# Four V copies of one attention unit move from VectorE to ScalarE, with a new stored instruction order

## The chip, the cores and the metric

The kernel runs on one core of a Trainium2 chip. The metric is the device time of one execution in microseconds (us). The engines are named as in the profile: PE (TensorE, matrix products), PEld (its weight loads), DVE (VectorE), ACT (ScalarE), POOL (GpSimd) and SP (SyncE, which here only issues DMAs).

## The reference

Two independent layers whose outputs are joined along the last axis. S = 2048 tokens, D = 640 channels, all in bf16.

```python
# A: a short filter, a gate, a long convolution over the tokens, a gate
k_shift = sum(k_pad[:, t:t+S, :] * shift_k[:, 3-t] for t in range(4))
kv = k_shift * v
y = irfft(rfft(kv, 2*S) * rfft(ssm_k, 2*S))[:, :S] + kv * ssm_D
a = q * y
# B: attention of 32 heads of 20 channels, in 4 segments of 512 tokens, with a memory
for s in range(4):
    p = softmax(qs @ ks.T * scale + causal_mask)
    a_dot = p @ vs
    a_mem = (phi(qs) @ M) / (phi(qs) @ z + 1e-6)
    o = g * a_mem + (1 - g) * a_dot
    M = M + phi(ks).T @ vs;  z = z + phi(ks).sum()
b = concat(o) @ wo
out = concat([a, b], axis=-1)
```

## The kernel before

**Layer A** is done in five convolutions of 128 channels each, `conv(dp)` with dp = 0 to 4. The filter and the gated input are transformed by matrix products with a table (`Wf`), ACT copies the products out of PSUM into the tile `F`, and DVE does the last butterflies (`Kh`, `Xh`), the complex product (`pq`, `Y`) and the first butterflies back. The inverse transform is again matrix products (`Y` with `Wi`). DVE multiplies the result by q (`outa`, or `vt` for the last convolution), and POOL issues its output DMA.

**Layer B** is done in eight units: unit u covers segment s = u // 2 and half = u % 2 of the heads (16 heads). Per unit:

- `project(u)`: PE multiplies the turned input `xT` by `wqkv`, in four blocks of 128 tokens. ACT copies K and Q of each block into `KQ`; V of each block is copied into `Va` by ACT or DVE. SP issues a DMA transposition of `KQ` into `KQT` for each block. `KQT` and `Va` exist once for each half, so unit u+2 writes over those of unit u. phi of K and Q is made by an exponential on ACT (`PP`) and two operations on DVE (`qabs`, `PP`); phi of Q is transposed by DMA into `PqT`. Then DVE reduces `KQT` to the largest key of each head and channel (`kam`, 2.28 us for one), makes the matrix `A` from it, PE multiplies it by |Q|, and ACT copies the product, a bound on the logits, into `bT`. Four small DMAs put it into spare rows of `KQT`.
- `attend(u)`: for four groups of four heads PE makes the logits in fills of 4 x 512 columns (below the diagonal, on it, and one joined fill for two groups), ACT takes the exponential of each fill in two instructions of 128 x 1024 (`ET`), PE multiplies by `Va` and by the memory `Mbd`, and DVE divides (`rr`, `o`, `o_s`).
- `project_out(s)`, once a segment is done: SP issues DMA transpositions of `o_s` into `xT`, PE multiplies by `wo`, the result is copied into `outb` (`kT` for the last segment) and written out.

**The order.** None of this runs in the order in which it is written. The functions only record operations; each one is kept with its engine and with the PSUM group that it uses. `ORDER` is a stored permutation of the 1501 operations and `BASE` the PSUM bank of each of the 470 groups; `rec.issue(order, base)` (lines 244 and 842) then emits the operations in that order. Every engine and every DMA queue works through its own part of the order strictly in sequence: an instruction that has to wait holds up all that stand behind it on the same engine. All instructions carry line 253 in the profile, the line of `issue` that emits them, so they are told apart by tile.

The engine that copies V is chosen in `project` by the list `LATE_V`:

```python
769  LATE_V = (6, 7)
590  self.evict(u in LATE_V, Va[:, t, :, 0:DH], g.ap[:, 0, 0:320].rearrange("p (h d) -> p h d", d=DH), g)
```

`evict` (line 351) emits a copy on DVE where its first argument is true, and on ACT otherwise. With `LATE_V = (6, 7)` the V copies of the last two units, eight of 32, are on DVE.

Of the kernel before, what the change touches and what calls it, by code (L numbers as in the profile page):

```python
# [21 lines left out]
S = 2048; D = 640  # L22
H = 32; DH = 20; NS = 4; L = 512
# [238 lines left out]
class Layer:  # L262
# [306 lines left out]
    def project(self, u):  # L569
# [5 lines left out]
        for t in range(4):  # L575
# [11 lines left out]
            with rec.one():  # L587
                for cc in range(5):
                    nc.tensor.matmul(g.ap[:, 0, 0:320], lhsT=xT[:, cc, tok], rhs=self.wqkv[:, cc, half, 2, :], start=(cc == 0), stop=(cc == 4), grp=g)
            self.evict(u in LATE_V, Va[:, t, :, 0:DH], g.ap[:, 0, 0:320].rearrange("p (h d) -> p h d", d=DH), g)  # L590
            rec.key = ("KT", u, t)
# [174 lines left out]
PEX = ()  # L766
TURNED = (0,)
LATE_W = (2, 3)
LATE_V = (6, 7)
EARLY_K = ()  # L770
EARLY_SK = (0, 1, 2)
PARTS = (0, 3, 4, 5)
SK_ACT, X_ACT, W_SP = (), False, ()
KQW, FW, WW = 1, 1, 1
ORDER = r"""
c-jrq(_$D16a>(ji@Hs1JGE`wscqY~ZQDt0+qP}n+Wmy{aMB_gq60{W^hkk-NQqR)fQ(3uKxD>r%!FVD0uUFGpol3EK*WRLD=Hy8qM|Y!X^;SkkreTf5Sfq!iBJ{EPzAA&9I+%0Vj~B#AO>P0C$b`~
q?268jcmw{<dQ<ZA%P^6ERt1X%Xegxl#)u)NFqrrMNkyQP#h&t5~WZYd5{<RkROFm7zI!eWl$Dzq&!kfpk$Qvl0h;_IV6+nsEy201JzImL8ysZNFqrkuEdjysDQ?3g63#})@XyesE2uIiulqD*`+=j
Ag4q|4rz!+C?EwT6k4Jc2FO5Zi+0E*xuvI!lU~vR?a>j1Bs2!eco{665C%~&Tt>(=>5SgeN2W?w43VKST}H|%nIIG8rc9E_l2^(~c_}BOWsKyJ?~+gQ%P{#NpQOKhmIyjU>PZ8sFF)m%bVEe#EB$1w
bb)IqEiB#914X2m%*I^I!3>!tGo=@z>j(KLs;1#Iy!J$Il#((s3;$%cKo`m)`GGmIK;{cIsxF4;JSi<jWwFf10))j9MA5mj6w9y>i_jO*v=4@&f>e}BvJsoG9wFF(eu$xKFaR-iIaXj8VrfHZEd4PU
#igW_kVaBNR-&fVlFitHfv7C2P(`XrH3^a?(o|NXnbejc7>?>vM+PAnYw-(pWdxebI&8%@w2<xCfnC^%FVa@pNqcE2t)z{N!e5E39b`XROGoJ>f3O<|aR_^H8l9z!bd_$h4+rpDzR42lE@AZy4&w-p  # L780
<0npF502tDj$tHD;uLzwSE<fO8lY!!4u2%B#@6#_pbfQ=#?i*QM!M)axqypUE1k5nhSo6JRa@$6X{GHnSbAzN?X5|)xhB;RX`%7-654Arjjstbu_n?EI#B!QXpBKe9ghi^gaJB8*UMx~!DS>=klY{}
<)Hk<KOB}7as@)8Q+XAKWR<LxrLs)IVTbILv6zTmvRn2@ZHD4<3C%DJ%c;1ANDN>&MrL?MXB0+dH13sYh`{Tp!-%|ro2bWIxQ$J+Pd3XI*(%%QF=BAP9Fe*_APw1w<8V}t$tgJ_+vN_9OMg8p=cFmm
%LVD7&GZRQ%Ly5xC#9R-Lk7Kz%W_4o$~76R8TF#H*6x}~oACiI$#uDpHhM#D$s^R~L&Rh(rqwu1%=Fqs8?y=1X#+OZq)f)x9I8nek8#;nQ?joP*O8i#XY?r&v7g?SVfqX&@Eq}(oGCN~Q|bu4C-)_}
zQik}W-6xAJ91ajFf9X_j_Fy0HThVc$U}J`kL0OjU`A$QX3eTubSFpYXdSO(^t=Ahe+nC`U-g@&)<Dh7G@6B3`Ba~2Exy5PY-LNn(YM;1Eg0IeX?D$_t(a4D=_mcD9odPw^|K~mdv;)6?aX|dUkhkK
&7+013yWw`eT#Q^j}IuOAMpvF@depAPP4Hs+p#OVvACAd!dg=Q=xcc+fAy8V)*Q^qvRY2x$~$Sz-E6}>%*EWy!%|vCcd@kQ<70iIFQmLy(3k&Lcl)jHw6a#ws#;AyXhof%m9(bT(%Sk(^RhUL@udW5
9j&X?)$Ex(msb+X!dMNhr|&hawXwEVUuj}fbec}o{A_BIG@^yKf}E-mteMT#`8rPvuqeY>5kA)!TFrv2idD5*R*1E2md@68*52l5b8BJKb*Ap+KF-iOR@Wj~fJL#W7TF5(r$)2I`b(E+H(RR9bh%E}
7241m*#cdtWmuMtZIPB>NtWh%U8SpaqXz4H3DFJOoojTHZq_ZjQrBuP9_A75(4E?Y`+0y>Se~U=mAiDSZr5$PTU%RC_GTY;v3`th`*gn^(1RMpz8ua&x>tvCogUU|+@nYJm>$;?+Q2$nSL<#gIG96t
QipLQNAZZB(jInN%W)t_Glq@fAok|~j^#FPXH6T&@tnZwc1~kj4U1>-t)A7l1lGaMYDa5nt?VEVF}v-ziOgY>nA1901@7P!PUdaBqepp+6<L{;IF&c`mfqF#oW@=@oxSZWFYp{svxyz&3|{0Jp5P_M
wm25odfF9zWeM%7zP9^z%@SE+dtle?hTXJ_n#3+?GCQvq^s?TydzRGtSYJEI%e<!jY!*-Px+b?+Hj}eCmrrdDm+^_Ev<I5P<}sC}wm=(XX>6eNw<}C*>1=>K)O&hgAL$EwX?g92=Ck~^fEg^KWwOkc
#nM|=o6jZuXrHWr6|_ZM%!RzlYrMgwyv|!JWH<TV3fl)OYQ;U5J+`}iXGN^6m9z48$8y_aK4b-}XnE|JeYav(+)CJ2D{0^Cxs|dfe9cGvVLvUKm9`RohxhoD&sfsm@FicdkQeq+{+usZ#wyuu4!4mu  # L790
!hTsTukBU5s+aRW_S-7keLmn=8)wUT%Wm5WuHs+&XK=dsO1|Y_8)BpEJ;&QSF1HUHZDVXL*Kq@<*>sy>Gi^PG+ALFFX`eXEX4^-W_tgyM8isI%O|Xf!k(;=gTlj@@tb#Z2NjBN0*i>6$%dC>mwRtw*
7T7{tWR-oXt+LhjnZfqP-dYW>=^?h(KHFD*V*y`h)xE6O^TqbXesGO#v`x0zw%AtNU<JLHueZ=1#=moi?X+FC+ba4t`^i1F-S*l(J78hGng@A(59bm5p*^yO-pIpyWRK#%S;y<T`9b^jKiwp%yBG1M
9?FY)L=W)N9?6q<GH>in{D?*K=pMskdKo`zNj;Xw_Bj5B&Ahp{_Ez4~TX-r@?QuPx$M*!D&=Yxb5A@@9!u~R)pR`k!-cxuc&+J(|t0(php3$>;8qe-I{E!{CbbieK5t7!sdUwz1xjeV$@w}eT^LsaM
<Lx|@gqE-}(l1+EALXO{qP6!9E~0YD!U-k3M3e~9$vgTL>*789v~~8V5=Np)bm{GVys!83{yxA5`U>yqy?l(1^+7(^m-!GM>cf1vkMkHZ-p|-XziP{Ul27oJKEkK?S&JkA5?P|iRG;iKe5TLx**?eT
`aGZJ)BT*Ev-5Vr=KBI)=!<-@2m2bo?x%dMpZC)q;+K7$FY%>*)Q|ZV-{k9ktKaa0e#p1^W<Tz${Dg1!Gk(~Q_-eo67yPDQ^=p38Z}|q_=zDyx@9>?z&oBB}-{t%Lw(s^!e!%|&2dC=h
"""
BASE = r"""
c-mD{0g?kD2#bL5{~sTQ==SOq9fSahyK#Po!0zQdCyI8rH`-TyvbMpKWA)vM0r!)6{K>nMk@ProvaQpG@Jf4jzB6jIXX)PQU2Ufdh-JM8Yk-jl*J)R;d%qY_vd)f;y(e>w)n-m-SH-x=HD-cSZFYRP
Fk*zxAP#s+?Q;%xvc=u>mYk&I!^6C|Ar3!mh_6v&`kVQ;c%GON=fl~DF?^X+G-;dMU5w-Lmf~_4OQ{v=G5Al-|M3C(L$URA-JE(fAO7YYq%<F9UFesG_=h|1DaDqvx2ayQPh+JU|Mi>7wugFo#$zU^
w@d5P)blnMnW;DTR)3e-c#4Orq^i2KSX?2cN|AUI;k~BRo57FnkTUo6FXG;>??nFrVeSTj  # L800
"""


# [69 lines left out]
```

## Time and profile before

| | |
|---|---|
| median of the timed runs | 292.07 us (291.34, 292.07, 292.85) |
| the profiled execution | 292.63 us |
| its span, first to last instruction | 290.9 us |
| mean granted TensorE clock | 0.998 |
| DVE busy | 263.3 us, 402 instructions |
| PE busy | 257.5 us, 4219 instructions |
| ACT busy | 252.1 us, 387 instructions |
| PEld busy | 193.1 us |
| POOL busy | 44.1 us |
| exponentials of the logits on ACT | 160 of 1064 ns |
| copies of V: ACT, DVE | 24 of 457 ns, 8 of 484 ns |

Busy time is the time in which an engine had at least one instruction under way. Instructions of one engine overlap at their ends, so the durations of a group add up to more than the engine's busy time. The span is that of one profiled execution; the rest of its 292.63 us lies around the first and last instruction.

### The profile page before, as it was taken

To read this page: it belongs to the slowest core of one execution; us is meant where nothing else is said; L and a number is where in the kernel's file an instruction comes from. 1 tells how busy PE (TensorE), PEld (TensorE's weight loads), DVE (VectorE), ACT (ScalarE), POOL (GpSimd) and SP (SyncE) were. 2 spreads that over 40 slices of the span, in tenths; PEclk is the share of its full clock that TensorE was granted. 3 is DMA by queue.
4 is the path that set the end of the run, shared out by engine and by line. 5 is a ranking of instruction groups with operands and counts; after the bars stand their busy time and mean duration, and the time that the engine had idled before them with its cause. 6 is when DMAs were issued, how large, how long until landed. Compare 5 with 4: busy or idle time off the path is not lost. (4 is left out here: it accounts for less than half of the span.)

```text
span 290.9 us, 9864 instructions
## 1 busy us (share of the span) xinstructions
PE 257.5 (89%) x4219; PEld 193.1 (66%) x4226; DVE 263.3 (91%) x402; ACT 252.1 (87%) x387; POOL 44.1 (15%) x71
## 2 busy tenths in 40 slices
PE   0899998889998989999889989999888887799895
PEld 0687765768677767787756777657756665476773
DVE  1279999999999999999999999999999999899654
ACT  0593899899998997999989989999989899899963
POOL 8300000001005000333000320201001400001620
PEclk9999999999999999999999999999999999999999
DMA  6999989996938498993794159983490119911332
GB/s 182 375 239 168 240 145 199 141 246 129 165 104 211 95 164 169 193 180 111 116 190 83 54 81 143 215 128 87 78 179 23 38 35 143 192 39 34 106 77 100
DMA packets 113500, 40.71 MB, mean 140 GB/s; under 512 B 105696, under 2 KB 111376, under 8 KB 113328
## 3 DMA queue, kind: packets, MB, share of 16 engines
q1 hardware_dynamic: 108624, 34.07, 60.9%
q0 software_dynamic: 2064, 4.76, 6.3%
q10 hardware_dynamic: 2768, 1.24, 1.5%
q8 instruction: 33, 0.54, 0.8%
q14 instruction: 11, 0.09, 0.1%
HBM read 14.11 MB, written 5.24 MB: 67 GB/s over the span
## 5 line engine op out<-in xcount | busy, mean ns | idle before, releaser
L253 ACT ACTIVATE ET<-ps 128x1024 bf16<-128x1024 f32 x160 | 155.8, 1064 | 6.8 <-PE ps L253 5.9
L253 PEld LDWEIGHTS <-xT 128*128 128x128 bf16 x640 | 59.7, 98 | 34.6 <-issue 12.2
L253 PE MATMUL ps<-wqkv,xT 128*128 128x320 bf16 x480 | 75.6, 303 | 4.7 <-ACT ET L253 1.4
L253 POOL DMA_DIRECT2D out_dram<-outa x32 | 22.4, 848 | 172.4 <-DVE outa L253 169.3
L253 ACT CAST F<-ps 128x512 bf16<-128x512 f32 x80 | 43.6, 628 | 4.9 <-DVE F L253 1.9
L253 PEld LDWEIGHTS <-ET 128*128 128x128 bf16 x1296 | 40.3, 96 | 3.9 <-issue 2.0
L253 PE MATMUL ps<-Va,ET 128*128 128x21 bf16 x1280 | 40.9, 172 | 0.7 <-ACT ET L253 0.5
L253 PE MATMUL ps<-KQT 32*128 32x128 bf16 (+2 forms) x896 | 35.0, 239 | 3.4 <-DVE o_s L253 1.0
L253 PEld LDWEIGHTS <-Wf 128*128 128x128 bf16 x320 | 29.9, 97 | 6.6 <-issue 2.3
L253 ACT CAST KQ<-ps 128x320 bf16<-128x320 f32 x64 | 27.4, 470 | 3.9 <-PE ps L253 2.6
L253 PE MATMUL ps<-wo,xT 128*128 128x320 bf16 x160 | 25.7, 299 | 2.3 <-DMA xT<-o_s 1.4
L253 PEld LDWEIGHTS <-KQT 32*128 32x128 bf16 x896 | 16.5, 92 | 14.2 <-issue 12.6
L253 PE MATMUL ps<-vt,Wf 128*128 128x256 bf16 x160 | 20.6, 272 | 0.7 <-DVE vt L253 0.7
L253 PE MATMUL ps<-kT,Wf 128*128 128x256 bf16 x160 | 20.9, 272 | 0.2 <-ACT F L253 0.2
L253 PE MATMUL ps<-Y,Wi 128*128 128x256 bf16 x160 | 20.3, 273 | 0.8 <-ACT ET L253 0.4
L253 PE MATMUL ps<-mright,mleft 32*128 32x128 bf16 x512 | 15.1, 216 | 6.3 <-ACT ET L253 3.0
L253 DVE TENSOR_TENSOR o<-ps,rr 128x640 bf16<-128x640 f32 x24 | 19.7, 820 | 0.7
L253 PE MATMUL ps<-skd,kr 128*128 128x128 bf16 (+3 forms) x133 | 19.0, 286 | 1.1 <-issue 0.4
L253 PEld LDWEIGHTS <-kr 128*128 128x128 bf16 x140 | 17.1, 145 | 3.7 <-issue 0.7
L253 PE MATMUL ps<-Mbd,PqT 128*128 128x84 bf16 x96 | 18.0, 201 | 0.8 <-ACT bT L253 0.4
L253 DVE TENSOR_TENSOR Y<-Y,pq 128x2048 bf16<-128x2048 bf16 (+1 forms) x20 | 18.7, 946 | 0.0
L253 DVE TENSOR_TENSOR pq<-Xh,Kh 128x2048 bf16<-128x2048 bf16 x15 | 18.3, 1218 | 0.3
(77 smaller groups left out, 359.3 us busy)
## 6 DMA issues: line engine op xcount, KB each, us to landing
vt<-in_A_v_dram SPq DMA_DIRECT2D x10, 256.0 KB
pq<-in_A_q_dram SPq DMA_DIRECT2D x10, 256.0 KB
out_dram<-outa POOLq DMA_DIRECT2D x32, 64.0 KB, 2.4
out_dram<-outb POOLq DMA_DIRECT2D x12, 160.0 KB, 2.6
ET<-in_A_ssm_k_dram SPq DMA_DIRECT2D x3, 512.0 KB
Wf<-c_wf SPq DMA_DIRECT2D x2, 512.0 KB
Wi<-c_wi SPq DMA_DIRECT2D x1, 1024.0 KB
kT<-in_A_ssm_k_dram SPq DMA_DIRECT2D x2, 512.0 KB
```

What stands on the lines that cost most here:

```text
L253: f(*[fix(a) for a in args], **{k: fix(v) for k, v in kw.items()})
```

## The change

`LATE_V` loses unit 6, so that its four V copies are emitted on ACT instead of DVE. With that comes another stored order of all operations and another choice of PSUM banks. The operations, their sizes, their tiles and everything else stay the same.

```diff
-LATE_V = (6, 7)
+LATE_V = (7,)
...
 ORDER = r"""
-(the stored permutation of 1501 operations)
+(another permutation of the same operations)
 """
 BASE = r"""
-(the stored PSUM bank of 470 groups)
+(another choice of banks)
 """
```

As the strings can't be read, here is what the new order moves where the prediction speaks of it, by engine (built from both kernels):

- ACT: the four V copies of unit 6 stand between the F copies of convolution 4 and the `bT` copy of unit 7, the first ahead of the `bT` copy of unit 6 and the last just ahead of the last exponential of unit 6's first group. The first `PP` exponential of unit 7 moves from ahead of `bT` of unit 6 to behind it. The 28 exponentials behind `bT` of unit 7 keep their order. At the start, the DMA of `wv` is issued behind the two exponentials of beta.
- DVE: the four V copies of unit 6 are gone. The reduction, the mask and `A` of unit 5 move ahead of the product of convolution 3; two operations of the product of convolution 4 move behind `A` of unit 7; a `PP` minimum and a `qabs` of unit 6 move ahead of the butterflies of convolution 4.
- PE: the logits below the diagonal of unit 5's second group move ahead of an inverse transform of convolution 3; `wo` products of segment 2 and first parts of `wo` products of segment 3 move by a few places near the end.
- SP: both transpositions of `o_s` of segment 2 move ahead of the two of `PqT` of unit 7; the fourth `KQT` transposition of unit 5 moves ahead of those of `o_s` of segment 1 and of x; `ident` is loaded behind the second x load instead of behind the first.
- POOL: the small constants are loaded in another order, and output DMAs move with what they write.

More of the change, by code (lines that the diff above doesn't have):

```diff
@@ L775 @@
 ORDER = r"""
[L776 to L795, printed above, removed]
+c-jrrgLW7S5Cy>9yLan0we8flZKt+v+qP{dwQbwBZR@>nm~$qrq!5vG5?#_uJc%qRC6#25jFMUcC9_PI88TBKCNU8~;z~pb5S6b&2``x>jpUL@5?>NX42dbRB(@}!#FA7JNiwM<NhG<XMHO+0h1`-&
@@ new lines @@
+(jkjfm8=p?vP%LaL=MR*$&mtCkQLeRT`Ef=e3QgThB%TEv5^XCP)G_(5h*GKq@a|N(vnB=N(m_`#iY38ll)Rf%1U}<KxU*yAmShilA^Z6M;$3AHKmqRlOU-saS;z0kqI@Vu{4o}(pnlxC@C)$rGnI#
+Hqu<`$~<W)4Wy~mlk8|Ap(Tv8k^&fjoM<LJkpsEV3%PL<c~B5-rJW2!d+8vZWE_U0qm0K0OhZ0&k<OAAQ6#F2L{}+<Q5cJ<7=*#-jXvlm6EF-DF&(2Z2K_Mwvt_R2M_H6dIdqr8=pnN(1HEJjW@0G5
+qc7^A9~!`I5<=Nz{6G;D!v}oC94U%V_>2e^(duKCL^m_qLM%d0`H3I$3;z(#!dnzuEK6ke|Af7zugt*$%*8@kB&ARqWw2D1$$VKL^AT3mqFNsrD#N6oR6s>6MkTD2Xf_Y9^%BEY$p%?28)b!Tl7?uE
+{!$zz@l!U-02wHQqy}oD7HXpoN+71Kl}4zHDu`uOQ4LKHgu1AXb+Sd8Vz@Lzh^&zjvRZ<rIliDR+MzvKpcVe2CB9*Z43@3Z0Y@dQZIkWN5u>CvcF0aSD7z%G?Unr!PTF9kbjBe$ES<1Vy5P8U#cnwu
@@ new lines @@
+-OwF><d+<gV{%eX$ZzR^J#t#A>sOqTB{(Bz<(x#a0Q-$UI4>9El7zM}wg&6a(pp(3>uj+tuB}BE>uPbVkzJI=*3Oz+Z|h@&t%3ElB$m`#STAd618lrZka!l~5?gyqXvwUDtwu*1XrpC}jFSX5S*Az`
+f^iUsa9OU%dL**3vH?`rNixWW*kNphsOkz#lT}!Wzw%Fp8nm`9#WI-I)8sbHuF7&um20vCJFyG9F;Vs)j7HF~8c}b^b-5`~HJXOfy$G$hB%I!s=o(&QXk?9~QM8T*XkFch$8rFhuo+vh72EJcj$l6;
+>QOY(V>pGTdKzc39p`WyZLPmGvpaGgXK(@CteM`Ei?}O~<RtpqLpgyAmeG3HWn95kTtj#3XRR%hwXy4HVwZ3O59GeY)LUq32{o3cwRD!=5^Hizp^3D<p0NhnSd-{&G|`vxN?yxOeIs!+jV9ID8du|K
+GQESlNMR{$q&<~q@?2g>DtnA4c!)=MinN+iQ)y}q)O0%BnrnK^Y+3Cd?&AUC>j=wY88oB*vrL*<v+5`tZDVb`J+&<Q%!FfXoTauj)=~qlmA26D_QN`AC;e*QEHrCsHp^}~ET`qQT-ILmS$^xFd-RRH
@@ new lines @@
+wU3tDYG^Ipss*f|6|th0#|qg;`6OTDt-O<BmQ4#=cKsl2wVig>E}B4#TMjK@IrTN(;In+P+?q@CXjko~`Lv|9);9XtUfFB=W4raQm9=tK-ty}+yq6bviMM!%=Xh+Ttc;bmC-w>xtb$dxDpu91S&&sU
+r}3RtvYJNLvf5V1s#{&FVfE~#g<^fnt6@0NK3G^zvI6?s!n2@8WCRw{!usCYuq~h43!7roY^qgZRerI#Hs6|Zo+-g*Y{&L&&K8_ywYW>?*iWm?aGY*+INN60UM-^g^p{0qHO{cbw!|h|ab0T5te6(n
+07heEF1HmHg>@OkMqFSG`5q;-q%N}38kGyJjF#2zy53gVY74dy+hCh)jjgouT29y6M%!$MwTJf99d<;kXeq6#TdbG%)}6M?`sh{*((Sg*_Ui%d#%g*{cUw(1<{{l@`|W@ow7z=CqI0P3wLNy!y6~8_
+W&<|iaa(7H?Su`}&K#^m^rQ{cL3+ea*+?CwUD=(dtrO2$3=Y>G9HFCijP}>DI!*`ZHjT&ljLDX4#ql~pdvT&xXAMr$$vQ>ru|E5-1NSolPwR2*&Fy+ZPwFYn&NEs;r|D6xs8e;i&d?k@t2x<EXX-4S
@@ new lines @@
+t#fsb9@F!7!Om+(UeL>WMX%X)J7?$gqFu7fcE#rDRl8w*8JqnWhjDp>H`$Z@dDCuLWxdAh9KetK#DpBgL`=;4+@TNnlmod`Z`&QaYxnHFC1Fxl(qz1-cNvTKcuAk|8B;MelQShB*h70{?-|H6Ov`jk
+!4F)fulSmInUDFIff<>J3p6vcFg@pMR=(g%F4D!iL>KCJUe#+_fCX8I*Y$?p(!wmtBFx1+ys7uKxaVeBmScH7)(R}f;(VyzSb`P#KufX|pXeif%o6^NPxY?e(`<aMFSIo8=rb+prTn$N(L#QQh5ajQ
+`E%Cx;Vi>S9Kj#_$&sw$w^-F*>MQ-lKfKM~9Lw<>$K|?0SLsR}%)cDPe>AWBf5k)iR!4I=#o_PtgO1@^U8mDHoijL-Ls{N8=xv?F6<o<-Ea$WNUO(!3oxn+4t)CgJA^J%x_(Xo;WKLlNujEr%**EGY
+{j5v4S-0q1F6BJV=K?O|GS1;5e$lV`P1oou26HtFctH<g4PV2xe8aa~$Fg42H*ym<a|^d}F}HC8ziVh;&oExyf9MYG<SrKTu)dpn7|tX3cJAd*-N$-f+RJ!-Kfv%F*$=XzH}YTVAfk9wZ|X%nq6c^#
@@ L796 @@
+uj`S#sMAAvV}Hm;tmZ-Pp2U-S6F<VE{H+x|nn(8-9@AraGmq`byt%jX*51-nd7!8ExE{~r`yWl<Ej*zo_mm#T6Zv0F>?e7O$9aP3J%wlT%$~)wdN$AQIXr`B^faE<5AiU&`acz<^PHZ`b9)}o>-jvt
+clS2l&5zL#3ZVhC^>#keNBL;K%qzS|#c5t*d+*@k5FQcG(K~r(@8UhYr$<CoL_>7MKyUBkeZ8Oe_W?f8m-`qGgO%RP2l-$h;zNCy5BC*5!pHhJAMa;4!6*7zUgad8?B}@5&oeBhcqB~q=|00}`YfOA
+0hr@+eV$+T>psor`vPC+i+r)K@m0Rg*ZUG*>#O~gAN9z%;lUo_SNyau^@D!MkNFng>YIGCpYtd<?-#huxBCX)=!gBdpYS7o#xM9uzv;L9s_*cNzSH;kHNWj={gUtXeZI?g`+h&*{{i6J>gE
 """
 BASE = r"""
-c-mD{0g?kD2#bL5{~sTQ==SOq9fSahyK#Po!0zQdCyI8rH`-TyvbMpKWA)vM0r!)6{K>nMk@ProvaQpG@Jf4jzB6jIXX)PQU2Ufdh-JM8Yk-jl*J)R;d%qY_vd)f;y(e>w)n-m-SH-x=HD-cSZFYRP
@@ L799 @@
-Fk*zxAP#s+?Q;%xvc=u>mYk&I!^6C|Ar3!mh_6v&`kVQ;c%GON=fl~DF?^X+G-;dMU5w-Lmf~_4OQ{v=G5Al-|M3C(L$URA-JE(fAO7YYq%<F9UFesG_=h|1DaDqvx2ayQPh+JU|Mi>7wugFo#$zU^
-w@d5P)blnMnW;DTR)3e-c#4Orq^i2KSX?2cN|AUI;k~BRo57FnkTUo6FXG;>??nFrVeSTj
+c-l=<0TRO?2#W~v{~r%R?7UtrB7_jE0XXn_vsQ;8%HCM?M0v7&S^L>p#c!S+o}I@7Ms@D4r;$)Gp@^V8p00sf7crc9MwDS=s?|&yHF(x6yH0Ws?gry9BUw2WW3-N#Z}ONm#jmTSSOx2Vh{m<m06m~(
+{C1_W?mAZ2UWyK343ANEGxHE<D{eFMb~-f{tzc%VtLc16<0QLaU(VhjT`#N4_s}-^OkSs+CdDt}7GH?d?e22EI=Ha#b?)MLgp``gDCyrMl70Vqy7JGXtAChBvq)*Uc(TMa^qrdpX*;h!{hN?o7&GHw
@@ L801 @@
+tt3i{H;DLh`eWHMAOBQvRU9pyx<da-NK4n9_J@fH9gpYQn>RIeLzCE{=>tDfMh1%
 """
```

## The prediction

> **What bounds the kernel now.** I read the busy times first, then the waits of single engines, then the stretch of the timeline that the change touches. Busy times (engine, us, share of the span, instructions):
>
> ```profile
> PE 257.5 (89%) x4219; PEld 193.1 (66%) x4226; DVE 263.3 (91%) x402; ACT 252.1 (87%) x387; POOL 44.1 (15%) x71
> ```
>
> Two engines are nearly full. The waits of DVE between 22 and 253 us (waiter, releaser: us, times, longest) are one line:
>
> ```profile
> DVE Kh L253 <- ACT F L253: 0.9, 1, 0.9
> ```
>
> It stands at 22.1 us. For 230 us after it DVE waits for nobody: DVE sets the pace, and the other engines' pauses follow from it. Busy time by stretch (start:end length, then engines with instruction counts) shows that this changes late:
>
> ```profile
> 25.00:230.00 205.00, 190.37 (x3022) 143.00 (x3028) 203.25 (x300) 187.34 (x297) 25.44 (x36) 1.00 0.74 141
> 230.00:250.00 20.00, 16.29 (x334) 11.09 (x333) 19.83 (x32) 19.63 (x24) 2.77 (x4) 1.00 0.62 99
> ```
>
> ACT is 91% busy up to 230 us and 98% from there. The timeline of ACT (start, us, instruction, count, the idle before it with its releaser):
>
> ```profile
> 210.58 1.07 ACT L253 CAST F<-ps 128x512 bf16<-128x512 f32 x2 [0.70 <-DVE F L253]
> ...
> 221.49 0.58 ACT L253 CAST bT<-ps 128x512 bf16<-128x512 f32 x1 [0.48 <-PE ps L253]
> ...
> 227.83 4.69 ACT L253 ACTIVATE ET<-ps 128x1024 bf16<-128x1024 f32 x5 [1.13 <-PE ps L253]
> ...
> 253.82 0.58 ACT L253 CAST bT<-ps 128x512 bf16<-128x512 f32 x1 [1.45 <-PE ps L253]
> 254.31 26.44 ACT L253 ACTIVATE ET<-ps 128x1024 bf16<-128x1024 f32 x28
> ```
>
> The last two rows matter most: after the bT copy of unit 7, 28 exponentials run in 26.44 us without a pause, to 280.75 us, and only the last projection follows. So the kernel's end is the time of that bT copy plus a nearly fixed tail, and the question is when ACT reaches it. PE's timeline shows what held ACT at 227.8 and 253.8:
>
> ```profile
> 226.43 1.03 PE L253 MATMUL ps<-Y,Wi 128*128 128x256 bf16 x8
> 227.40 0.40 PE L253 MATMUL ps<-KQT 32*128 32x384 bf16 x8
> ...
> 251.44 0.85 PE L253 MATMUL ps<-wo,xT 128*128 128x320 bf16 x5 [1.37 <-DMA xT<-o_s]
> ```
>
> The first wait is PE's order: an inverse transform of the convolution stands ahead of the logits that ACT needs. The second is a transposition that PE waits 1.37 us for. SP's queue says why it is late:
>
> ```profile
> 238.27 7.23 SPq L253 DMA_TRANSPOSE KQT<-KQ  x4
> 245.60 1.27 SPq L253 DMA_TRANSPOSE PqT<-PP  x1
> 246.97 1.42 SPq L253 DMA_TRANSPOSE xT<-o_s  x1
> 248.49 1.39 SPq L253 DMA_TRANSPOSE PqT<-PP  x1
> 249.93 1.44 SPq L253 DMA_TRANSPOSE xT<-o_s  x1
> ```
>
> SP issues without a break, and PE starts 0.07 us after the last one ends (251.37 to 251.44).
>
> **The copies.** Four copies of unit 6's V go from DVE to ACT. The copies in the trace, min/median/max ns:
>
> ```profile
> L253 ACT CAST Va<-ps x24: 406/440/553, 22.2 to 180.5; 128x320 bf16<-128x320 f32 x24
> L253 DVE CAST Va<-ps x8: 481/482/488, 221.1 to 251.9; 128x320 bf16<-128x320 f32 x8
> ```
>
> These durations overlap the next instruction; what a full engine pays is the distance from start to start, 0.41 us on DVE and 0.32 on ACT in back-to-back rows of the trace. DVE loses 4 x 0.41 = 1.6 us, ACT gains 4 x 0.32 = 1.3 us. [...]
>
> **DVE by the new order.** I add start-to-start durations of rows of before along both orders. Up to the matrix A of unit 7 (the last product of DVE that the bT copy needs) the new order has 2.4 us less on DVE: 1.6 from the copies, the rest work of convolution 4 that now stands behind. As DVE has no idle time to lose, A can come at 251.95 - 2.4 = 249.6 us. Earlier units: A of unit 1, 2, 3 and 4 stand 0.6, 1.2, 1.0 and 1.2 us later, of unit 5 6 us and of unit 6 0.6 us earlier. A later A of units 1 to 4 costs nothing: the bT copy stands 0.8 to 2.6 us behind A, and the unit's first logits many us behind that (unit 4: bT at 158.8, logits at 178).
>
> **ACT from 210.6 us to the bT copy of unit 7.** In both orders this stretch holds the same 8 F copies (0.49), 8 KQ copies (0.33), 2 PP (0.66), 32 exponentials (0.914) and one bT copy (0.47): 3.9 + 2.6 + 1.3 + 29.2 + 0.5 = 37.6 us; after, the four V copies too, 38.9. Before it took 253.82 - 210.58 = 43.24 us, so 5.6 us were idle: 0.64 (F, for DVE, at 213.1), 0.56 (KQ, 215.2), 0.48, 1.13, 0.24 (236.3) and 1.45 in rows of the timeline, and 1.1 in gaps too short for rows. After:
> - The start. The F copies wait for DVE's subtraction of X of convolution 4, which has 0.65 us more work ahead of it (a PP minimum and a qabs pulled forward): 211.2.
> - 0.64 becomes about 0.2: five copies now stand ahead of the F copy that waited, not three.
> - 0.56 becomes about 0.3: the KQ copy stands further back.
> - 0.48 goes: A of unit 6 is 0.6 us earlier.
> - 1.13 goes: PE now has the logits ahead of the inverse transform, and ACT has a PP of 0.66 us in between. The transform and its outa product are later by one 0.40 logits block; what reads outa is an output DMA that nothing waits for.
> - 1.45 goes. On SP both xT transpositions now stand ahead of the two PqT, 1.27 + 1.39 = 2.7 us earlier; the PqT have until the values of unit 7 at 271 us, and the two q loads that also move are read at 265. ACT's new copies make it arrive later as well.
>
> Left: 0.2 + 0.3 + 0.24 + 1.1 = 1.85 us idle. The bT copy starts at 211.2 + 38.9 + 1.85 = 251.9 us, 1.9 earlier.
>
> **Who else must be there by 251.9.** The transpositions of unit 7's K and Q start when the last logits of unit 5 are done. ACT lets these through at 211.2 + 25.1 (work up to there) + 1.5 idle = 237.8 us, 0.5 earlier than before; SP needs 7.2 us, so 245.0, and xT is there at 247.9, 3.5 us earlier. DVE comes to its first read of KQT at about 245.2. It will wait on the way: it reaches the third reciprocal of unit 5 2 us earlier, but PE's values only end at about 239.0, some 1.4 us after DVE is there. So 1.4 of DVE's 2.4 us turn into a wait, A comes at 250.8 to 251.0, and PE's bound product, behind the values of unit 6 (249.7 to 251.2, after the copy of V and the last exponential of unit 6's first group), at 251.2. Everything meets within 0.7 us: ACT, PE and DVE arrive together, and further gains on DVE would be worth nothing.
>
> **The tail.** The 28 exponentials have the same order. Before the last logits PE does one more wo block (0.64 us, with 0.5 us of slack ahead of it: +0.15); behind the last values one block of three products fewer is left on a PE that sets the end there (278.05 to 287.68 on the chain of waits): -0.37. Together -0.2.
>
> **The head.** The load of wv is issued by ACT after the beta exponentials instead of at 5.01 us: 0.37 us of issue on an ACT that runs full from 13.8 us to the F copies DVE waits for; and ident, for which PE starts at 5.03 us, is issued one x load later (0.42). The second x load is earlier, and ACT has a pause of 0.57 us at 13.2. Between a gain of 0.4 and a loss of 0.8, I take +0.2, the value of a half-hidden issue.
>
> **Sum.** -1.9 - 0.2 + 0.2 = -1.9 us on a profiled execution of 292.63 us (span 290.9): 290.7. That execution is 0.56 us over the median of 292.07, so on the median's scale I forecast 290.2 us.
>
> **Rival 1: ACT becomes the bound and the gain is gone.** Of the pauses only the 1.13 us goes, which is in PE's order; the others come back elsewhere, because ACT, at 98% in 230 to 250 us, gets 1.3 us more and the values of unit 6 now wait for V copies that stand late in ACT's order. Then the bT copy moves by +0.65 + 1.3 - 1.13 = +0.8, the end by +0.8 - 0.2 + 0.2: 292.9 us, no change. For it: three engines meet within 0.7 us, so a small delay of any one is felt. Against: the 1.45 us hangs on SP's order, which is improved whatever ACT does. [...]
>
> **Rival 2: slower, through the transpositions of unit 5.** The new order pulls DVE's reduction of unit 5 6 us forward, to about 180.4 us, ahead of the product of convolution 3. The reduction needs the fourth K/Q transposition, which SP issued at 183.61 to 184.92 us, behind xT and x. It now stands ahead of these and should be done by about 178.5 (start at 169.6, 0.7 for a PP exponential that ACT now does first, 6.3 for the four, 1.9 for a PqT among them). If it is late, DVE, in order, stands still, and all that follows with it; it decides once it lands after 180.4, and where it lands at 184.9 as before the price is 4.5 us less a gain of at most 1.9: 294.7 us. Against it: two us of margin.
>
> **Rival 3: more gain.** If the short gaps go too (1.1 us) and the head gains 0.4 instead of losing 0.2: 288.5 us; it needs A of DVE at 249.6, without the wait at unit 5.
>
> **Chances.** A measurement of this kernel can tell about 0.5%, 1.5 us, from no change. Forecast 0.42, rival 3 0.08: faster 0.50. Rival 1: 0.27. Rival 2: 0.23. The range reaches from 288.8, short of rival 3, to 294.0, within rival 2; faster cases alone lie in 288.5 to 290.6.
>
> **What would show it.** 28 V copies on ACT and 4 on DVE in place of 24 and 8; the bT copy of unit 7 starts at 251.9 with no wait over 0.5 us for xT; no 1.1 us wait of ACT near 227; a DVE wait of about 1.4 us for PE at the reciprocals of unit 5; 28 exponentials in 26.4 us after bT. A bT copy after 253.8, or DVE waits of several us before 210, would make the forecast wrong.

## The result, and the profile after

The changed kernel takes 291.60 us in the median, the kernel before 292.58 us beside it: ratio 0.9954, 95% interval [0.9935, 0.9973], that is 1.35 us less (0.8 to 1.9). Two later measurements gave 0.9948 and 0.9941. The forecast was 1.9 us less. The gain is real and lies at the edge of the 0.5% that was named as the resolution.

Busy times and DVE's waits between 20 and 253 us in the profile after (290.99 us, span 289.2; columns as before):

```profile
PE 258.5 (89%) x4226; PEld 195.3 (68%) x4226; DVE 262.0 (91%) x398; ACT 254.0 (88%) x391; POOL 42.5 (15%) x71
```

```profile
DVE Kh L253 <- ACT F L253: 1.7, 1, 1.7
DVE outa L253 <- issue: 0.2, 1, 0.2
```

Four instructions have gone from DVE to ACT, and DVE still waits for no other engine after 22 us. The row of busy time from 230 to 250 us shows ACT, at 19.63 of 20 us before, now with no pause at all:

```profile
230.00:250.00 20.00, 16.09 (x343) 11.14 (x342) 19.76 (x29) 20.00 (x26) 2.75 (x4) 1.00 0.70 113
```

The copies of V (min/median/max ns, first to last start): 28 on ACT, 4 on DVE.

```profile
L253 ACT CAST Va<-ps x28: 426/444/582, 21.7 to 248.2; 128x320 bf16<-128x320 f32 x28
L253 DVE CAST Va<-ps x4: 483/485/486, 244.1 to 249.7; 128x320 bf16<-128x320 f32 x4
```

ACT's timeline around the two `bT` copies, and SP's between 236 and 258 us:

```profile
213.74 1.56 ACT L253 CAST F<-ps 128x512 bf16<-128x512 f32 x3 [0.57 <-PE ps L253]
...
221.76 0.67 ACT L253 CAST bT<-ps 128x512 bf16<-128x512 f32 x1
...
251.39 0.59 ACT L253 CAST bT<-ps 128x512 bf16<-128x512 f32 x1
251.95 1.94 ACT L253 ACTIVATE ET<-ps 128x1024 bf16<-128x1024 f32 x2
255.25 24.28 ACT L253 ACTIVATE ET<-ps 128x1024 bf16<-128x1024 f32 x26 [1.35 <-PE ps L253]
```

```profile
236.79 6.72 SPq L253 DMA_TRANSPOSE KQT<-KQ  x4
244.26 2.91 SPq L253 DMA_TRANSPOSE xT<-o_s  x2
247.27 1.36 SPq L253 DMA_TRANSPOSE PqT<-PP  x1
248.73 1.31 SPq L253 DMA_DIRECT2D pq<-in_A_q_dram  x2
250.09 1.95 SPq L253 DMA_TRANSPOSE PqT<-PP  x1
252.15 3.63 SPq L253 DMA_DIRECT2D KQT<-bT  x4
```

The `bT` copy of unit 7 comes 2.4 us earlier, without its wait for `xT`. (In this pair of profiles 0.8 us of the 2.4 stands already at `A` of unit 0, 31.9 us against 32.7; see the head below.) But behind it stands a pause of 1.35 us that was not there before: the 28 exponentials take 28.1 us from the start of the `bT` copy to their end, before 26.9. So of 2.4 us half is given back at once. The tail, from the last exponential to the end of the last `kT` copy, is 0.4 us shorter (6.97 against 7.38).

The same places in all profiled executions, worked out from the timeline rows (us; the runs are told of below, and the last column starts at the end of the last exponential):

| kernel | profiled execution | start of `bT` of unit 7 | from there to the end of the last exponential | from that end to the end of the last `kT` copy |
|---|---|---|---|---|
| before | 292.63 | 253.82 | 26.92 | 7.38 |
| after | 290.99 | 251.39 | 28.14 | 6.97 |
| after, again | 291.98 | 252.40 | 28.13 | 6.96 |
| after, third | 290.84 | 251.31 | 28.06 | 6.94 |
| order only | 293.72 | 255.25 | 27.04 | 6.93 |
| copies only | 292.45 | 253.64 | 26.93 | 7.38 |
| copies only, again | 293.25 | 254.44 | 26.92 | 7.38 |
| PqT ahead of xT | 290.48 | 251.65 | 27.04 | 7.29 |
| last PqT behind the rows | 290.45 | 251.41 | 27.28 | 7.27 |
| the same, again | 290.04 | 251.11 | 27.27 | 7.17 |
| transform ahead | 291.27 | 252.00 | 27.83 | 6.95 |
| three edits in the old order | 291.85 | 252.89 | 26.92 | 7.39 |
| all V copies on ACT | 293.34 | 253.54 | 28.34 | 6.94 |
| one PqT late in the old order | 294.81 | 254.29 | 28.63 | 7.39 |

One program places its `bT` copy up to 1.1 us apart in two executions (251.31 and 252.40), while the last two columns repeat within 0.1. So small differences in the third column are not read from one profile; the timed medians decide those. In the last two rows PE's granted clock falls to 0.50 behind the `bT` copy, so their fourth column is no measure of the pause.

### The profile page after: what moved, and what is told of

Read it like the earlier page. It is cut to its first block, busy times and chain, and to the rows that moved or that the text cites. A ratio compares the mean times of both kernels' runs of the same rounds, so it can differ in the third digit from the quotient of the medians.

```text
span 289.2 us, 9883 instructions
## 1 busy us (share of the span) xinstructions
PE 258.5 (89%) x4226; PEld 195.3 (68%) x4226; DVE 262.0 (91%) x398; ACT 254.0 (88%) x391; POOL 42.5 (15%) x71
## 5 line engine op out<-in xcount | busy, mean ns | idle before, releaser
L253 PEld LDWEIGHTS <-xT 128*128 128x128 bf16 x640 | 60.5, 99 | 32.2 <-issue 10.8
L253 ACT CAST F<-ps 128x512 bf16<-128x512 f32 x80 | 43.0, 614 | 4.2 <-DVE F L253 1.6
L253 PE MATMUL ps<-skd,kr 128*128 128x128 bf16 (+3 forms) x140 | 20.9, 301 | 1.1 <-ACT ET L253 1.0
L253 PE MATMUL ps<-mright,mleft 32*128 32x128 bf16 x512 | 14.4, 219 | 6.5 <-ACT ET L253 3.4
```

The costliest lines, as they stand in the source:

```text
L253: f(*[fix(a) for a in args], **{k: fix(v) for k, v in kw.items()})
```

## The experiments

Theory, as in the prediction: DVE, PE and ACT arrive at the `bT` copy of unit 7 together, and the new order gains by taking ACT's pauses away. Rivals: the order of SP and PE alone is the gain (rival a in the expectations); DVE alone sets the pace, and the gain is the 1.6 us of copies taken off it (rival b).

### Which part brings the gain

The changed kernel again, unchanged:

> The changed kernel once more, for its interval and for one row: in its first profiled execution the 28 exponentials behind the bT copy of unit 7 took 27.6 us instead of 26.4, with one pause of 1.35 us at 253.9 for which no product was late, while a DMA issue on SP took 1.88 us instead of 0.5. If the pause belongs to the order, it is there again (1.0 to 1.5 us, same exponential); if it belongs to that one execution, the exponentials run in 26.4 to 26.6 us and the span is about 1.1 us shorter, 288.1. Time by both: 1.0 to 1.9 us under the kernel before.

291.44 us, ratio 0.9948 [0.9922, 0.9975]. The pause is there again, at the same exponential, 1.42 us. It belongs to the kernel, not to one execution.

The new order, with the copies back on DVE:

```diff
-LATE_V = (7,)
+LATE_V = (6, 7)
```

> New order, the four copies of unit 6's V left on DVE. Theory (three engines arrive together, each part takes one late arrival away): DVE gets 4 x 0.41 = 1.6 us back ahead of A of unit 7, so A ends at about 252.0, the bT copy starts at 252.6 to 253.0 behind the bound product, with ACT waiting 1 us or more for it; time 1.2 us over the changed kernel, 0 to 0.5 us under the one before. Rival a (the order of SP and PE is the gain, the copies only load ACT): ACT has 1.3 us less, bT copy at 250.1 to 251.4, time 0 to 1.2 us under the changed kernel. Rival b (the relief of DVE is the whole gain): as the kernel before.

292.93 us, ratio 0.9993 [0.9966, 1.0020]: the new order alone brings nothing that can be measured. DVE's waits that are new from 20 to 253 us, and what stands at `bT` in the timelines of PE and ACT:

```profile
DVE rr L253 <- PE ps L253: 0.6, 1, 0.6
DVE qabs L253 <- DMA KQT<-KQ: 0.6, 1, 0.6
```

```profile
252.88 0.84 PE L253 MATMUL ps<-wo,xT 128*128 128x320 bf16 x5 [1.14 <-DVE Va L253]
255.25 0.59 ACT L253 CAST bT<-ps 128x512 bf16<-128x512 f32 x1 [1.48 <-PE ps L253]
```

ACT, with less to do, waits 1.48 us for a product of PE, and PE, a little ahead of that product, 1.14 us for a V copy on DVE: the last of the four that were put back. The time is what rival b expected and close to the theory's; it refutes rival a. The `bT` copy comes later than the theory (252.6 to 253.0) or rival b (253.8) had it, in a profile 0.8 us over the run's median.

It is not `A` that holds `bT`. In all 14 profiles PE starts the product for `bT` right behind the last values of unit 6's first group, 0.6 to 3.4 us after `A` has ended. In the changed kernel (`A` on DVE, the product on PE):

```profile
250.07 0.29 DVE L253 TENSOR_TENSOR A<-sel,kam 128x128 bf16<-128x128 bf16 x1
250.94 0.40 PE L253 MATMUL ps<-qabs,A 128*32 128x512 bf16 x4
```

So DVE reaches `bT` through what PE waits for ahead of those values, the V copies among it. In this run DVE does the four copies at the places that the new order has for ACT. Whether the new order with the copies at other places of DVE's order would do as well as the change was not tried.

The old order, with the copies on ACT, twice:

```diff
-LATE_V = (6, 7)
+LATE_V = (7,)
```

> Old order, the four copies of unit 6's V on ACT. Theory: A of unit 7 comes up to 1.6 us earlier on DVE, but PE still waits for the second xT transposition behind both PqT on SP, and ACT has 1.3 us more; bT copy of unit 7 at 253.8 to 254.6, time 0 to 0.8 us over the kernel before. Rival b (the relief of DVE is the whole gain): bT copy at 252.2, time 1.3 to 1.6 us under the kernel before, as the changed kernel. Rival a: ACT's 1.3 us in full, 0.8 to 1.3 us over the kernel before.

> Old order with the four copies on ACT, once more: the first run's time was 1.0 us under the kernel before, while its profiled execution showed A of unit 7 1.0 us earlier but the bT copy only 0.2 us earlier, behind xT. If xT gates the bT copy in most executions, the time is 0 to 0.4 us under the kernel before; if the gain of the first run is real, 0.7 to 1.2 us under it.

291.97 us, ratio 0.9966 [0.9942, 0.9990], and 291.98 us, ratio 0.9968 [0.9936, 1.0000]: 0.9 to 1.0 us under the kernel before, both times. The theory had expected 0 to 0.8 us over it, rival b 1.3 to 1.6 under it. The profiled executions don't show where the gain is: they lie 0.5 and 1.3 us over the medians of their runs, and both have the `bT` copy behind a wait of about 1 us. Both were slowed just ahead of it: PE's granted clock is 0.50 at 250 to 252 us. The `wo` block takes 1.51 us in both, where it takes 0.85 in the kernel before, and from its start to `bT` it is 3.1 us, in ten of the others 2.4. So at least 0.7 us of the lateness of `bT` is the clock's:

```profile
250.51 1.51 PE L253 MATMUL ps<-wo,xT 128*128 128x320 bf16 x5
253.64 0.59 ACT L253 CAST bT<-ps 128x512 bf16<-128x512 f32 x1 [1.01 <-PE ps L253]
```

What follows: the copies alone give 0.9 to 1.0 us, the order alone 0.2 (-0.6 to 1.0), both together 1.35 to 1.7. By the timed runs the four copies carry the change, in the old order as in the new (there 1.3 us, with intervals that just overlap). How they do it shows in the new order alone, in the waits above; in the old order it is not shown. Whether the order adds some half a microsecond, these intervals don't settle.

### The two terms of order: SP and PE

SP's order of unit 7, put back to one `PqT` ahead of each `xT`:

```diff
 KQT KQT KQT KQT
-xT  xT  PqT pq  pq  PqT
+PqT xT  PqT xT  pq  pq
 KQT<-bT (4 row copies)
```

> The changed kernel with SP's old order at one place: the two PqT transpositions of unit 7 stand again ahead of one xT transposition each. Theory: the second xT lands 2.7 us later, at about 249.9 instead of 247.2; PE's wo block, now at 249.0, starts with a wait at about 250.0, the values of unit 6 and the bound product behind it about 0.9 us later; bT copy at 252.1 to 252.6, time 0.7 to 1.1 us over the changed kernel. Rival b (DVE alone decides, and DVE doesn't read xT): no difference, within 0.3 us.

290.96 us, ratio 0.9928 [0.9906, 0.9951]: not slower than the changed kernel, as the theory had it by 0.7 to 1.1 us, but, if anything, 0.5 us faster. PE's timeline shows the wait that comes back:

```profile
249.27 0.85 PE L253 MATMUL ps<-wo,xT 128*128 128x320 bf16 x5 [0.45 <-DMA xT<-o_s]
```

It is 0.45 us, not 1.37. SP starts the four `KQT` transpositions at 236.56 us here, 1.7 earlier than before, so `xT` is early enough even behind both `PqT`. And the pause behind the `bT` copy is gone (27.04 us instead of 28.1).

PE's order, with the inverse transform of convolution 3 ahead of the logits of unit 5 again:

```diff
-logits unit 5, 2nd group | inverse transform 3 | V of unit 6
+inverse transform 3 | logits unit 5, 2nd group | V of unit 6
```

> The changed kernel with PE's old order at one place: the inverse transform of convolution 3 stands again ahead of the logits of unit 5. By the prediction's 1.13 us term ACT waits again, about 0.8 us at 226 to 228, but every wait of ACT there ends up in the 1.2 us by which ACT can be late before the bT copy of unit 7: if ACT sets that copy, time 0.5 to 1.1 us over the changed kernel. Rival (DVE sets it, as the runs with and without the four copies suggest): A of unit 7 stays at 250.1, ACT catches up, time within 0.3 us of the changed kernel.

291.95 us, ratio 0.9964 [0.9935, 0.9994]; ACT's wait is back, as in the prediction's term:

```profile
227.18 1.94 ACT L253 ACTIVATE ET<-ps 128x1024 bf16<-128x1024 f32 x2 [0.85 <-PE ps L253]
```

From the first F copy to the `bT` copy of unit 7 ACT takes 40.5 us, in the three profiles of the changed kernel 40.1, 40.4 and 40.1. But those three hold another wait, of 0.5 to 0.6 us for PE near 214 us, that this one doesn't have; two later profiles without either wait (the last `PqT` behind the row copies, below) take 40.1 and 39.9. So between 0.1 and 0.7 us of the 0.85 is left at `bT`. The time is 0.3 to 0.7 us over the changed kernel's, inside the intervals. Both agree with a term of about half its size; neither the theory's range nor the rival's is settled.

The kernel before with three edits alone, the copies on ACT, `xT` ahead of `PqT`, and the logits ahead of the transform. The early logits overwrite PSUM banks from which one exponential of unit 5 is still to read, so that one works on other values, with the same instructions:

```diff
-LATE_V = (6, 7)
+LATE_V = (7,)
 (SP)
-PqT xT  PqT xT
+xT  xT  PqT PqT
 (PE)
-inverse transform 3 | logits unit 5, 2nd group
+logits unit 5, 2nd group | inverse transform 3
```

> The kernel before with three edits alone: the four copies on ACT, both xT transpositions ahead of both PqT on SP, the logits of unit 5 ahead of the inverse transform on PE. The run with the copies alone had a wait of 1.0 us ahead of the bT copy of unit 7 and one of 0.8 us near 227. If these three edits are what the new order brings, both waits go: bT copy at 252.5 to 252.9, time 1.4 to 2.0 us under the kernel before. If the rest of the new order is needed, it is as the run with the copies alone, 0.7 to 1.1 us under the kernel before. If the row copies again follow a PqT closely, the pause of 1.4 us eats the gain: 0.4 to 0.6 us under it.

292.25 us, ratio 0.9972 [0.9947, 0.9996], no better than the copies alone. `bT` stands at 252.89 without a wait; the wait near 227 us is still there:

```profile
227.11 5.61 ACT L253 ACTIVATE ET<-ps 128x1024 bf16<-128x1024 f32 x6 [1.04 <-PE ps L253]
```

This wait comes from the edit itself. With the copies alone ACT runs five exponentials ahead of the wait near 227 us, here four: the fifth is the one whose bank is overwritten, so it now has to wait for the early logits. The new order can move them because it also gives half of them other banks (6 and 7 in place of 2 and 3). So this run doesn't tell what the early logits are worth with banks of their own, nor whether the rest of the new order is needed.

### The pause

The changed kernel with the last `PqT` behind the row copies, twice, with the changed kernel beside it the second time:

```diff
 xT  xT  PqT pq  pq
-PqT
 KQT<-bT (4 row copies)
+PqT
```

> The changed kernel with the last PqT transposition of unit 7 behind the four row copies KQT<-bT on SP instead of ahead of them. The pause of ACT (1.35 and 1.42 us in two executions of the changed kernel, none in the run with PqT ahead) stands where the row copies follow that transposition by 0.1 us. Theory (transposition and copies collide): the pause goes, 28 exponentials in 26.4 to 26.6 us, time 1.0 to 1.4 us under the changed kernel. Rival (the pause belongs to the place in ACT's program, whatever SP does): it is there again, time as the changed kernel.

> The changed kernel with the last PqT transposition behind the row copies, once more, beside the changed kernel itself on the same chip: 0.9 to 1.2 us under it if the pause is the difference (28 exponentials in 26.4 to 27.3 us against 27.6 to 28.2), no difference if the first comparison was chance.

> The changed kernel a third time, as the measure for its neighbours: 1.0 to 1.7 us under the kernel before, the pause of 1.1 to 1.4 us behind the bT copy of unit 7 again.

290.42 us, ratio 0.9911 [0.9884, 0.9938], and 289.82 us, ratio 0.9917 [0.9881, 0.9952]; the changed kernel beside the second 291.08 us, ratio 0.9941 [0.9910, 0.9972]. SP's rows of the second, and ACT's:

```profile
251.72 2.27 SPq L253 DMA_DIRECT2D KQT<-bT  x4
254.03 1.27 SPq L253 DMA_TRANSPOSE PqT<-PP  x1
```

```profile
255.84 22.53 ACT L253 ACTIVATE ET<-ps 128x1024 bf16<-128x1024 f32 x24 [0.24 <-PE ps L253]
```

In the changed kernel beside it the transposition starts at 250.10 us, the row copies follow at 251.99 and take 3.60 us, and ACT's pause is 1.26 us, as in the rows of the profile after.

With the transposition just ahead, the four row copies take 3.6 us to issue and ACT stands still for 1.3; with it behind, 2.27 us and 0.24. By the ratios that place in SP's order costs 0.7 us beside the changed kernel, and 0.9 to 1.3 us where the first run is held against the changed kernel of other measurements; the intervals of the two kernels still overlap, but both runs and all profiles say the same. This version, 2.4 to 2.6 us under the kernel before, is the fastest of all that ran. The pause was seen in all four profiles in which the row copies start 0.1 us behind that transposition (1.35, 1.42, 1.26, and 1.09 us in the run with the transform ahead), and in none of the two with the transposition behind them, nor with `PqT` ahead of `xT`, nor in the order-only run, where the copies start 1.4 us behind it. A slow PE is not its cause: the granted clock is 1.00 from 252 to 258 us in all four.

The same closeness made in the old order:

```diff
 PqT xT
-PqT xT  pq  pq
+xT  pq  pq  PqT
 KQT<-bT (4 row copies)
```

> The kernel before with one edit: SP's second PqT transposition of unit 7 stands behind the last xT and the two q loads, right ahead of the row copies KQT<-bT, as in the changed kernel. The last xT lands some 1.4 us earlier, so the bT copy of unit 7 comes at 252.4 to 253.0 instead of 253.8. If a row copy close behind a transposition makes the pause of ACT, it appears here too, in the old order: the 28 exponentials take 27.4 to 27.9 us instead of 26.4, and the time is 0 to 0.5 us under the kernel before. If the pause belongs to the new order, the exponentials take 26.4 us and the time is 0.8 to 1.4 us under it.

292.49 us, ratio 1.0002 [0.9971, 1.0032]. As a test of the pause it failed: the row copies came 1.5 us behind the transposition and issued in 2.25 us, so the two were not close. The `bT` copy came at 254.29, not at 252.4 to 253.0. The profiled execution is also 2.3 us over its median, for another reason that a window shows (columns as above, the granted clock third from the end), with the wait in front of it in PE's timeline:

```profile
254.00:258.00 4.00, 3.86 (x91) 2.85 (x88) 3.62 (x6) 3.06 (x4) 0.00 (x0) 0.50 0.45 84
```

```profile
251.61 0.85 PE L253 MATMUL ps<-wo,xT 128*128 128x320 bf16 x5 [1.63 <-DMA xT<-o_s]
...
257.34 2.66 PE L253 MATMUL ps<-wo,xT 128*128 128x320 bf16 x10
```

### Who sets the pace afterwards

The step of the change doubled, all V copies on ACT:

```diff
-LATE_V = (7,)
+LATE_V = ()
```

> The changed kernel with the four copies of unit 7's V on ACT too, so the step of the change doubled. DVE gets 1.6 us less ahead of A of unit 7 (248.5), ACT 1.3 us more between 242 and 250. If ACT and DVE arrive together, as the prediction had it, ACT becomes the bound: bT copy of unit 7 at 252.4 to 252.7, time 0.8 to 1.3 us over the changed kernel. If DVE alone still sets the pace: bT copy at 250.2 to 250.6, time 0.8 to 1.2 us under it.

291.56 us, ratio 0.9962 [0.9933, 0.9990]: no further gain, by the ratio 0.2 to 0.6 us over the changed kernel, inside the intervals. DVE, relieved once more, ends `A` of unit 7 at 249.7 us and then waits:

```profile
DVE outb L253 <- PE ps L253: 1.8, 1, 1.8
```

while ACT reaches the `bT` copy at 253.54 us, without a pause: 41.5 us after its first F copy, 1.1 to 1.5 us more than in the changed kernel, about the 1.3 us of four copies. So in this profile, which lies 1.8 us over the run's median, ACT has become the bound, and further relief of DVE brings nothing. That four more copies cost their 1.3 us is not shown: the times differ by less than half of it.

## Why the prediction was right, and where it was not

**Right.** The kernel is faster, by a little less than forecast, and it got there at the place named: 28 and 4 copies, no wait for `xT` ahead of the `bT` copy of unit 7, none of 1.1 us near 227, the copy at 251.4 where 251.9 was written, its product behind the values of unit 6 at 250.9 where 251.2 was written. Rival 2 did not happen: DVE's reduction of unit 5 starts at 180.9 us without a wait, and SP has issued its fourth transposition by 177.5. Rival 1 did not happen at this step, but is what the doubled step met: three engines close together, and ACT first to be full.

**"28 exponentials run in 26.44 us without a pause, and only the last projection follows".** This is the step that failed most: 28.1 us instead of 26.9 from the `bT` copy, +1.2. The forecast took the order of the exponentials, which did not change but for the two halves of seven fills that swap places, for the whole story, and cost the late `PqT` at nothing, because nobody reads it before 271 us. It paid with what stands behind it on SP: the row copies, and ACT at the same moment.

**"1.45 goes", through SP's order.** The wait went, but not for that reason: with the old order of `xT` and `PqT` it is 0.45. Its larger part went because the `KQT` transpositions start 0.9 to 1.7 us earlier in these profiles. The reading under it, that `xT` is there 0.07 us after SP's last issue ends, was a coincidence of one profile: in the old order with one `PqT` moved away, SP has issued both `xT` by 250.09 us and PE starts at 251.61.

**"1.13 goes", through PE's order.** It went. But with the transform ahead again only 0.1 to 0.7 us of the 0.85 us wait is left at `bT`, and the time tells 0.3 to 0.7. Here the pause of an engine that later meets another was not a full term of the sum.

**"Up to A the new order has 2.4 us less on DVE".** Between A of unit 0 and A of unit 7 DVE takes 218.2 us (218.7 and 218.0 in the other two profiles), before 218.9. The instructions taken away weigh what was said (2.73 us out: the four copies and one operation of the product of convolution 4, not two; 0.40 in: a V copy of unit 7); but the 315 that stay, 216.2 us before, take 217.6 to 218.3. What lies between two starts depends on the neighbour (0.72 or 0.60 us for half products of one kind, as the last section shows), and the sum had carried each duration over to its new place. The wait of 1.4 us at unit 5's reciprocals is absent for the same reason: DVE was not early.

**The head and the tail.** The tail gained 0.4 instead of 0.2, but 0.1 to 0.2 in the three profiles of the new order whose `bT` came near 251.4 and that have no pause. The head (+0.2 forecast) can't be told: A of unit 0 starts between 31.2 and 32.9 us in five profiles of the old order and between 31.5 and 32.4 in nine of the new.

**The sum.** In the profiled executions: forecast -1.7 at the `bT` copy (-1.9 and +0.2), 0 in the exponentials, -0.2 in the tail; measured, in the mean of three executions, -2.1, +1.2 and -0.4. That the total came near is in part luck: the start of `bT` was earlier than forecast, the pause later gave half of it back, and two of the terms (1.13 and 1.45) were not what they were taken for. The copies themselves, which the sum took as 1.6 us less against 1.3 more, are the part that carries the gain: they leave DVE, before the change the engine with the largest busy share (91%).

## What to carry to other kernels

Where one engine has no idle time for most of the span, ask first what leaves it, and count pauses of the others only where the chain of waits ends in them. Of a transfer that moves later, price what is issued right behind it on its queue, not only who reads it. And after a step that worked, try half and double of it, since the next engine may be full already. Compare the granted clock of the timed executions too, before the rest of a difference is put down to the order.

## What the runs showed of the hardware that was not expected

**A DMA transposition just ahead of small copies on the same queue.** With the `PqT` transposition 0.1 us ahead, one of the four row copies takes 1.88 us to issue instead of 0.50 (1.95, 1.84 and 1.67 in the three others). The DMA view of the profile after, for the microsecond from 251 to 252, then for the half from 253.5 to 254:

```profile
DMA packets 1118, 0.28 MB, mean 282 GB/s; under 512 B 1118, under 2 KB 1118, under 8 KB 1118
```

```profile
DMA packets 11, 0.00 MB, mean 6 GB/s; under 512 B 11, under 2 KB 11, under 8 KB 11
```

The next two halves have 22 and 373. So packets of 256 bytes (1102 of the 1118), the size that the transpositions move here, nearly stop for a microsecond and then go on; single ones that begin just before take up to 1.86 us instead of 18 ns. SP's issue and ACT's exponential both go on within 0.06 us of each other. That moving the transposition takes ACT's pause from 1.26 to 0.24 us is shown. Why ACT, whose product had been ready for 1.35 us, stands still with it is open: no record in the trace ties that exponential to the transfers.

**Two neighbours on DVE that depend on each other.** The times of four DVE starts in the profile after:

```profile
227.80 0.68 DVE L253 TENSOR_TENSOR Kh<-Kh 128x1024 bf16<-128x1024 bf16 x1
228.52 0.69 DVE L253 TENSOR_TENSOR Kh<-F 128x1024 bf16<-128x1024 bf16 x1
229.13 0.69 DVE L253 TENSOR_TENSOR outa<-ps,pq 128x512 bf16<-128x512 f32 x1
229.73 0.68 DVE L253 TENSOR_TENSOR Kh<-F 128x1024 bf16<-128x1024 bf16 x1
```

The first, whose successor depends on it, takes 0.72 us to the next start, the others, of the same kind and nearly the same duration, 0.61 and 0.60. Over both profiles, the half products `Xh` (128x1024) take 0.72 us where the next instruction reads or writes over what they touch (9) and 0.60 where it does not (31). In the new order 26 of the 315 instructions got such a successor and 22 lost one, +3.1 and -2.5 us; the remaining 1.0 us of the 1.6 is spread over many small waits. In these two profiles a successor that depends on such a half product thus costs 0.12 us each time.

**The clock after a wait.** In the run with the late `PqT` in the old order PE waited 1.63 us ahead of 251.6; its granted clock then was 0.50 from 254 to 258 us, and ten `wo` products took 2.66 us instead of 1.52. PE's busy time in the 4 us up to 254 doesn't tell the runs apart: 2.39 us here, 2.63 in the kernel before with 1.00 from 254 to 258, and 3.41 in the run with all copies on ACT with 0.50 at 256 to 258. Why the clock fell was not shown.

**Granted clock and time.** Such stretches are not equally frequent in the two kernels. Of the 101 executions of the kernel before that were timed beside the experiments 81 have a mean granted clock of 0.998 or more, of the changed kernel's 44 only 7, of the copies alone 10 of 24, of the order alone 1 of 12. Executions with less take longer (means): before 292.5 against 294.1 us, copies alone 291.4 against 292.4, changed 290.6 against 291.4. At the higher clock the changed kernel is thus 1.9 us under the kernel before, as much as was forecast, and the copies alone 1.2. In the profile after one such stretch is at 208 to 210 us (0.54), and ACT's wait of 0.57 us at 213.74 follows it; the five profiles of the new order with at most 0.63 there have that wait (0.5 to 0.7 us), the four with 1.00 don't. This is a comparison after the fact of few executions; what in the new order lowers the clock was not tried.
